# An adaLN block with a spectral mixer and a SwiGLU layer: more planes added on VectorE, a weight row loaded by itself, a split last tile, and new step orders

## The chip, the cores and the metric

The kernel runs on one core of one Trainium2 chip. Its time is the device time of one execution in microseconds, the median of several runs. The engines are named as in the profile: PE is TensorE (matmuls; PEld its weight loads), DVE is VectorE, ACT is ScalarE, POOL is GpSimd, and SP is SyncE, which here only issues transfers. Sixteen DMA engines move the data.

## The reference

The input x has 2048 tokens of 640 channels, in bf16. Six vectors of 640 (shift, scale and gate for two halves) come from a small condition vector c and a matrix w_mod.

```python
mod = (_silu(c) @ w_mod).reshape(c.shape[0], 6, 1, -1)      # sa, ca, ga, sb, cb, gb
h = _layernorm(x, axis=-1) * (1 + ca) + sa
X = rfft2(h over tokens and channels) * (w_r + 1j * w_i)     # w_r, w_i: 2048 x 321
x = x + ga * irfft2(X)
h = _layernorm(x, axis=-1) * (1 + cb) + sb
x = x + gb * ((_silu(h @ w_gate) * (h @ w_up)) @ w_down)     # 640 -> 1728 -> 640
```

## The kernel before

The tokens lie in 16 tiles t of 128. The work is one straight program. Within each stage a string, the plan, lists the steps, and the order of that list is the order in which each engine gets its instructions; engines run their own queues in order and wait for one another by semaphores. The plans were written out ahead of time. A step is a letter and a number: `S12` is the step S for tile 12.

**First stage (functions under ps1, to about 35 us).** For each tile t: `T` turns x on PE (x_sb is loaded in pairs of tiles by `lx`), `h` copies the turned tile out of PSUM, `G` and `d` compute the norm's sums, `p`, `r` and `s` the scaled Fourier table (POOL), `B` and `Z` the channel transform, `S` (s1) the first step of the token transform, and `A` (acopy) copies its result to A_sb; A12 is copied in three pieces. Which engine copies is set by the names in ON_DVE: named ones go to DVE, the others to ACT. `lca`, `ca`, `cb` and `rs` handle the scale ca, `lsa`, `ms`, `sacs`, `mh` and `sh` the shift sa. Before the first T, PE runs small matmuls on c and 12 matmuls on an identity tile (L400).

**The spectral weights.** Wb holds w_i in plane 0 and w_r in plane 1, as 128 partitions x 16 slots x 321 columns. `lW` (L223) loads one plane, `lf` (fix_rows, L210) then overwrites parts of partition 0 with other rows of the same matrix, and `J` (turn_w, L438) reads all of it on PE, reversed; `Je` (L443) copies that to Wq, and `N` makes the negated plane. `J2` and `J3` read w_i, `J0` and `J1` w_r:

```python
ws = [w.rearrange("(k2 k1) l -> k1 k2 l", k1=P) for w in (A_w_i, A_w_r)]
"lW": lambda a: nc.sync.dma_start(Wb[:, a, :, 0:321], ws[a])
nc.sync.dma_start(Wb[0:1, a, lo:hi, m:m + 63], ws[a][0:1, k:k + hi - lo, m:m + 63])   # lf
wv = Wb[:, 1 - h // 2, :, 1:257].rearrange("p k (m l) -> p k m l", m=2)               # J, step h
```

All these loads are issued by SP in the order of the plan: the x and G loads, `lsa`, `lW1`, `lW0`, `lK` (Ktab), the fix rows, `lga` (columns of the gate ga, wm_g), then the transposes `B`/`Bl` of A_sb by DMA.

**Second stage (to about 64 us).** 17 units u of four columns each. `T` and `t` turn units 0, 1 and 16 on PE (t2, L498; the others come by DMA transposes), `X` (stage_x) transforms, `Xe` copies out, `P` and `R` multiply by the weights on DVE (L562), giving two planes. For a unit in ADDED, `a` (add_planes, L570) adds the planes on DVE and `Y` turns the sum with 5 transposes (L580, L581); for the others `Y` adds and turns with 10 matmuls on an identity (L586, L590). `y` (L599) copies Y out, `E` transforms back, `e` (L634) copies to Ep, and `m` writes mirrored columns. ADDED is (0, 2, 4, 6, 8, 10, 12, 14).

**Third stage and FFN.** `s` (L720), `V`, `d`, `x` form x1, followed by the second norm and the turned tiles h2T. Then for each of four groups sc of four tiles: 13 blocks of `ffn_mm` (L812), silu on ACT, a product on DVE (ffn_mul, L821), and `down` (L934), which accumulates 13 blocks for each half of each tile, plus `down13`. `fold` (L848) multiplies a block of w_down by the gate gb on DVE; in the first group it runs between products, by the table `folds`.

**The last half tile** (sc 3, tl 3, h 1) uses two PSUM parts of 160 columns: x is added by two identity matmuls (L931), the 13 blocks go alternately to both parts, ACT copies one part and DVE the other (L946), and one store takes both.

Of the kernel before, what the change touches and what calls it, by code (L numbers as in the profile page):

```python
# [11 lines left out]
BF16 = mybir.dt.bfloat16  # L12
# [18 lines left out]
def _tables():  # L31
# [70 lines left out]
    "012021021021021020210210212012010210210210210"  # L102
)
SLOTS2 = (
    "0301321032103213012301230210321023102301230213201231032103210231023102310231320132012310321020130323"
    "013120132013201320132013201320132013201320132013201320132013201320132"
# [4 lines left out]
def adaln_block_kernel(  # L111
# [39 lines left out]
    one11 = const.tile([1, 1], BF16, name="one11")  # L151
    identb = const.tile([P, 128], BF16, name="identb")
# [29 lines left out]
    g_row = [dram.tile([1, D], BF16, name=n) for n in ("ga_row", "gb_row")]  # L182
    nc.vector.memset(one11[:], 1.0)
# [28 lines left out]
    def load(o, i):  # L212
        return lambda _: nc.sync.dma_start(o, i)
# [4 lines left out]
    def load_g(g):  # L218
# [4 lines left out]
             "lW": lambda a: nc.sync.dma_start(Wb[:, a, :, 0:321], ws[a]), "lK": load(Ktab[:], K_dram), "lKI": load(KIt[:], KI_dram),  # L223
# [3 lines left out]
        "A12 Xe0 Xe9 Xe10 Xe16 e1 e14 e15 f0 f1 f2 f3 f4 f6 f7 f8 f9 g15 h0 t0 t1 y0 y2 y4 y8 y12 y14 y16 "  # L227
# [55 lines left out]
    with tc.tile_pool(name="ph1", bufs=3) as ph1, \  # L283
# [111 lines left out]

        cps = Tt[:, 330:330 + NC5]
        for k in range(NC5):
            nc.tensor.matmul(cps[:, k:k + 1], lhsT=c_row[0:1, k * 128:(k + 1) * 128], rhs=one11[:], start=True, stop=True)
        for _ in range(12):
            nc.tensor.matmul(Gt[:, 0:128], lhsT=identb[:], rhs=identb[:], start=True, stop=True)  # L400
# [44 lines left out]
        def negate(i):  # L445
# [30 lines left out]
    with tc.tile_pool(name="ph2", bufs=2, reuse_waits="tile") as ph2:  # L476
# [186 lines left out]
        def loads(i):  # L663
# [11 lines left out]
        ADDED = (0, 2, 4, 6, 8, 10, 12, 14)  # L675
        MCOLS = ((0, 15), (15, 31), (31, 47), (47, 59), (59, 63))
        plan = (
# [30 lines left out]
    def ring(name):  # L708
        return take2(name)
# [109 lines left out]
    def ffn_mul(AT, fc):  # L819
        gu, sg = gus.pop(fc)  # L820
        nc.vector.tensor_tensor(AT[:, fc, :], gu[:, 1, :], sg[:], ALU.mult)  # L821
# [28 lines left out]
    def at_of(sc):  # L850
# [31 lines left out]
    folds = {8: (4, 5, 6), 9: (7,), 10: (8,), 11: (9, 10, 11), 12: (12, 13)}  # L882
    for sc in range(4):
        AT = at_of(sc)
        if sc:
            ffn13(sc)
        for fc in range(0 if sc else done, NFC - 1):
            ffn_mm(sc, fc)
            ffn_silu(fc)
            if sc == 0:  # L890
                for f in folds.get(fc, ()):
                    fold(f)
            ffn_mul(AT, fc)
            if fc == 2:
                ffn_mul13(sc, AT)
            if sc == 1 and fc == 4:
                ln2_power(8, 16)
            if sc < 3:
                n0 = 4 * (sc + 1)
                if fc in (9, 10):  # L900
                    ln2_xn(n0 + 2 * (fc - 9))
                    ln2_xn(n0 + 2 * (fc - 9) + 1)
                if fc == 10:
                    ln2_turn(sc + 1)
        if sc < 3:
            ln2_affine(sc + 1)
        acc = [t_[:, h, 0:320] for t_ in [ring("oa") for tl in range(4)] for h in range(2)]
        if sc == 3:
            acc[7] = [ring("ob")[:, 0, 0:160] for _ in range(2)]

        def early(tl, h):
            return tl > 1 and not (sc == 3 and tl == 3 and h)

        def parts(tl, h):
            o = acc[2 * tl + h]
            return [(o[q], 160 * q, 160) for q in range(2)] if isinstance(o, list) else [(o, 0, 320)]

        def down13(tl, h):
            r = slice(64 * h, 64 * h + 64)
            for o, d0, n in parts(tl, h):  # L920
                nc.tensor.matmul(o, lhsT=AT[r, 13, tl * 128:(tl + 1) * 128], rhs=Wd_sb[r, 13, h * 320 + d0:h * 320 + d0 + n],
                                 start=early(tl, h), stop=not early(tl, h))

        def x_half(tl, h):
            return x1[:, 4 * sc + tl, 320 * h:320 * h + 320]

        def down(tl, h):
            ps = parts(tl, h)
            if len(ps) > 1:
                for o, d0, n in ps:  # L930
                    nc.tensor.matmul(o, lhsT=identb[:], rhs=x_half(tl, h)[:, d0:d0 + n], start=True, stop=False)  # L931
            for fc in range(NFC - 1):
                for o, d0, n in ps:
                    nc.tensor.matmul(o, lhsT=AT[:, fc, tl * 128:(tl + 1) * 128], rhs=Wd_sb[:, fc, h * 320 + d0:h * 320 + d0 + n],  # L934
                                     start=(fc == 0 and not early(tl, h) and len(ps) == 1), stop=(fc == NFC - 2 and early(tl, h)))

        xos = {}

        def x_out(tl, h):
            t = 4 * sc + tl  # L940
            if h == 0:
                xos[tl] = ph4.tile([P, D], BF16, name="xo", bufs=3)
            ps = parts(tl, h)
            if len(ps) > 1:
                for (o, d0, n), copy in zip(ps, (nc.scalar.copy, nc.vector.tensor_copy)):
                    copy(xos[tl][:, h * 320 + d0:h * 320 + d0 + n], o)  # L946
            else:
                nc.vector.tensor_tensor(xos[tl][:, h * 320:(h + 1) * 320], ps[0][0], x_half(tl, h), ALU.add)  # L948
            if sc == 3 and tl == 3:
                nc.sync.dma_start(out_v[:, t, h * 320:(h + 1) * 320], xos[tl][:, h * 320:(h + 1) * 320])  # L950
            elif h == 1:
                nc.sync.dma_start(out_v[:, t, :], xos[tl][:])

        for tl in range(2):
            for h in range(2):
                down(tl, h)
        for tl in range(4):
            for h in range(2):
                if tl < 2 or early(tl, h):
                    down13(tl, h)  # L960
        for tl in range(2):
            for h in range(2):
                x_out(tl, h)
        for tl in range(2, 4):
            for h in range(2):
                down(tl, h)
                if not early(tl, h):
                    down13(tl, h)
                if sc == 3 and tl == 3:
                    x_out(tl, h)  # L970
            if sc < 3 or tl == 2:
                for h in range(2):
                    x_out(tl, h)
# [48 lines left out]
```

## Time and profile before

| What | us |
|---|---|
| median of 3 runs | 263.67 (262.97 to 264.32) |
| the profiled execution | 262.81 |
| its span | 261.0 |
| PE busy | 252.7 (97% of the span) |
| DVE busy | 141.1 (54%) |
| ACT busy | 118.6 (45%) |
| POOL busy | 26.4 (10%) |

The span runs from the first to the last instruction in the trace. In the rows of groups the numbers behind the count are busy us, the mean of one in ns, and the idle time before them with what ended it. A row of the timeline has its start, its length, engine, line and operation; a row of the chain has start, length and what it was. Shares are means over stages with different limits, so the stages are read one by one.

### The profile page before, as it was taken

To read this page: it belongs to the slowest core of one execution; us is meant where nothing else is said; L and a number is where in the kernel's file an instruction comes from. 1 tells how busy PE (TensorE), PEld (TensorE's weight loads), DVE (VectorE), ACT (ScalarE), POOL (GpSimd) and SP (SyncE) were. 2 spreads that over 40 slices of the span, in tenths; PEclk is the share of its full clock that TensorE was granted. 3 is DMA by queue.
4 is the path that set the end of the run, shared out by engine and by line. 5 is a ranking of instruction groups with operands and counts; after the bars stand their busy time and mean duration, and the time that the engine had idled before them with its cause. 6 is when DMAs were issued, how large, how long until landed. Compare 5 with 4: busy or idle time off the path is not lost.

```text
span 261.0 us, 5283 instructions
## 1 busy us (share of the span) xinstructions
PE 252.7 (97%) x2168; PEld 159.9 (61%) x2172; DVE 141.1 (54%) x353; ACT 118.6 (45%) x212; POOL 26.4 (10%) x57
## 2 busy tenths in 40 slices
PE   6899999999999999999999999999999999999995
PEld 5788666888995444466544456744445664444664
DVE  5799989999887664933243343234344322433122
ACT  5689879996993669420222222032223103222000
POOL 4289700000010001300000000000000000000000
PEclk9999999999999999999999999999999999999999
DMA  7999499999599100141100040210005011000011
GB/s 243 381 356 298 112 175 160 176 330 379 153 370 303 38 14 1 23 77 57 58 10 3 0 92 11 75 35 10 3 0 100 30 48 35 10 3 0 0 53 50
DMA packets 36798, 27.88 MB, mean 107 GB/s; under 512 B 19493, under 2 KB 34214, under 8 KB 36646
## 3 DMA queue, kind: packets, MB, share of 16 engines
q1 hardware_dynamic: 36762, 27.54, 37.1%
q8 instruction: 17, 0.28, 0.5%
q14 instruction: 7, 0.06, 0.1%
q10 hardware_dynamic: 12, 0.00, 0.0%
HBM read 20.13 MB, written 2.62 MB: 87 GB/s over the span
## 4 chain that ended last, share of the span: by engine, by line
PE 79%; DVE 12%; ACT 3%; issue 2%; DMA 2%; SPq 1%; DVEq 0%; ACTq 0%
PE gu L812 37%; PE oa L934 21%; PE va L720 3%; DVE PP L562 3%; DMA x_sb<-in_A_x_dram 2%; PE oab L733 2%; PE gu L799 2%; ACT junk L744 2%; PE aps L353 1%; DVE AT L821 1%; PE aps L354 1%; PE z L340 1%; DVE Z L345 1%; PE gps L308 1%; DVE late L848 1%
## 5 line engine op out<-in xcount | busy, mean ns | idle before, releaser
L821 DVE TENSOR_TENSOR AT<-gu,sg 128x512 bf16<-128x512 f32 x52 | 35.7, 690 | 63.3 <-ACT sg L817 63.3
L812 PE MATMUL gu<-h2T_all,Wg 128*128 128x512 bf16 x260 | 64.6, 379 | 0.1
L812 PE MATMUL gu<-h2T_all,Wu 128*128 128x512 bf16 x256 | 63.7, 379 | 0.1
L817 ACT ACTIVATE sg<-gu 128x512 f32<-128x512 f32 x52 | 30.7, 596 | 67.9 <-PE gu L812 65.1
L934 PE MATMUL oa<-late,AT 128*128 128x320 bf16 x403 | 56.3, 299 | 0.5 <-DVE AT L821 0.5
L934 PEld LDWEIGHTS <-AT 128*128 128x128 bf16 x429 | 40.7, 98 | 17.6 <-issue 1.1
L812 PEld LDWEIGHTS <-Wu 128*128 128x128 bf16 x260 | 25.4, 98 | 30.7
L812 PEld LDWEIGHTS <-Wg 128*128 128x128 bf16 x260 | 25.3, 98 | 29.9
L948 DVE TENSOR_TENSOR xo<-oa,late 128x320 bf16<-128x320 f32 x31 | 13.4, 484 | 34.6 <-PE oa L934 18.2
L801 ACT ACTIVATE sg<-gu 64x512 f32<-64x512 f32 x4 | 2.4, 591 | 36.0 <-PE gu L799 36.0
L736 DVE SCALAR_TENSOR_TENSOR late<-oab,x_sb 128x640 bf16<-128x640 f32 x16 | 12.8, 822 | 6.4 <-PE oab L733 5.0
L333 POOL TENSOR_SCALAR Gs<-Gtab,rstd 128x256 bf16<-128x256 bf16 x15 | 13.9, 928 | 8.1 <-DVE rstd L323 7.1
L345 DVE SCALAR_TENSOR_TENSOR Z<-rtile,vm,z 128x640 bf16<-128x640 f32 x16 | 13.9, 871 | 0.1
L744 ACT ACTIVATE junk<-late,mean 128x640 bf16<-128x640 bf16 x16 | 13.3, 828 | 0.3
L367 ACT CAST A_sb<-aps 128x650 bf16<-128x650 f32 x15 | 10.6, 706 | 2.1 <-PE aps L354 2.0
L727 ACT CAST VT<-va 128x640 bf16<-128x640 f32 x16 | 10.2, 699 | 1.9 <-PE va L720 1.8
L720 PE MATMUL va<-Htab,Ep 128*128 128x128 bf16 x160 | 10.6, 219 | 0.1
L720 PEld LDWEIGHTS <-Ep 128*128 128x128 bf16 x160 | 9.5, 118 | 0.4 <-DVE Ep L278 0.3
L353 PE MATMUL aps<-Z,Gs 128*128 128x325 bf16 x32 | 9.2, 303 | 0.2 <-DVE Z L345 0.2
L354 PE MATMUL aps<-Z,Gs 128*128 128x315 bf16 x32 | 9.2, 298 | 0.0
L540 ACT CAST X<-xps 128x640 bf16<-128x640 f32 x13 | 8.5, 710 | 1.1 <-PE xps L531 0.8
L562 DVE TENSOR_TENSOR PP<-X,Wb 128x768 bf16<-128x768 bf16 x16 | 8.7, 550 | 0.0
(291 smaller groups left out, 307.0 us busy)
## 6 DMA issues: line engine op xcount, KB each, us to landing
x_sb<-in_A_x_dram SPq DMA_DIRECT2D x8, 320.0 KB
out_dram<-xo SPq DMA_DIRECT2D x15, 160.0 KB, 2.2
Wu<-in_B_w_up_dram SPq DMA_DIRECT2D x1, 2080.0 KB
late<-in_B_w_down_dram SPq DMA_DIRECT2D x1, 2080.0 KB
wm_g<-in_w_mod_dram SPq DMA_DIRECT2D x2, 800.0 KB
Wb<-in_A_w_r_dram SPq DMA_DIRECT2D x1, 1284.0 KB
Wb<-in_A_w_i_dram SPq DMA_DIRECT2D x1, 1284.0 KB, 13.0
Wg<-in_B_w_gate_dram SPq DMA_DIRECT2D x1, 1280.0 KB, 8.1
```

The costliest lines, as they stand in the source:

```text
L333: e.tensor_scalar(Gss[t][:, 0:2], Gtab[:, t], rstd1[:, t:t + 1], None, ALU.mult)
L345: nc.vector.scalar_tensor_tensor(Zs[t][:].rearrange("p r q -> p (r q)"), rv, vm[:, t, 1:2], held.pop(("z", t))[:, 0:D], ALU.mult, ALU.add)
L353: nc.tensor.matmul(o, lhsT=Gs[:, a, :], rhs=Z[:, :, 0:NL], start=True, stop=False)
L562: nc.vector.tensor_tensor(bass.AP(o.tensor, o.offset, [o.ap[0], [4 * NI, 2], [2 * NI, 2], [4, n], [1, 4]]), bass.AP(xi.tensor, xi.offset, ...
L720: nc.tensor.matmul(vf[:, 128 * r:128 * r + 128], lhsT=Ep[:, t, 65 - 65 * g:193 - 65 * g, r], rhs=Htab[:, t, g, :], start=(f == 1 and r in ...
L736: nc.vector.scalar_tensor_tensor(x1[:, t, :].rearrange("p (a r) -> p a r", r=NR), VTs.pop(t).rearrange("p (r a) -> p a r", r=NR), 1.0, x_s ...
L744: nc.scalar.activation(junk[:], x1[:, t, :], ACT.Square, scale=-1.0 / D ** 0.5, bias=mean2[:, t, 1:2], accum_out=sq2[:, t:t + 1])
L812: nc.tensor.matmul(o, lhsT=w_[:, c5, fc * 128:(fc + 1) * 128], rhs=h2T(sc, c5), start=(c5 == 0), stop=(c5 == NC5 - 1))
L817: nc.scalar.activation(gus[fc][1][:], gus[fc][0][:, 0, :], ACT.Silu)
L821: nc.vector.tensor_tensor(AT[:, fc, :], gu[:, 1, :], sg[:], ALU.mult)
L934: nc.tensor.matmul(o, lhsT=AT[:, fc, tl * 128:(tl + 1) * 128], rhs=Wd_sb[:, fc, h * 320 + d0:h * 320 + d0 + n], start=(fc == 0 and not ear ...
L948: nc.vector.tensor_tensor(xos[tl][:, h * 320:(h + 1) * 320], ps[0][0], x_half(tl, h), ALU.add)
```

## The change

Eleven units are in ADDED: 1, 5, 9 and 13 come in, 0 goes out. ON_DVE changes: A11 in place of A12, h3 in place of h0; of the second stage's copies Xe0, Xe9, Xe10, Xe16, e1, e14 and the first half of e15 go to ACT, and the y copies of added units except y8 go to DVE. A tile `hot` is zeroed first on DVE, and PE runs 11 matmuls on it before the small ones on c and 11 after (instead of 12 on the identity). `lw` loads partition 0 of a weight plane, and `lW` the other 127. The folds of blocks 12 and 13 follow the last product of the first group, and the others are spread anew. The last half tile is computed part by part: each part takes its 13 blocks and down13, one DVE operation that adds x, and its own store; no identity matmuls. The three plans and the orders of the PSUM slots are new.

```diff
+    hot = const.tile([P, 128], BF16, name="hot")
+    nc.vector.memset(hot[:], 0.0)
...
-             "lW": lambda a: nc.sync.dma_start(Wb[:, a, :, 0:321], ws[a]), ...
+             "lw": lambda a: nc.sync.dma_start(Wb[0:1, a, :, 0:321], ws[a][0:1]),
+             "lW": lambda a: nc.sync.dma_start(Wb[1:P, a, :, 0:321], ws[a][1:P]), ...
...
-        "A12 Xe0 Xe9 Xe10 Xe16 e1 e14 e15 f0 f1 f2 f3 f4 f6 f7 f8 f9 g15 h0 t0 t1 y0 y2 y4 y8 y12 y14 y16 "
+        "A11 f0 f1 f2 f3 f5 f6 f7 f8 f9 g15 h3 t0 t1 y1 y2 y4 y5 y6 y9 y10 y12 y13 y14 y16 "
...
+        def keep_busy(n):
+            for _ in range(n):
+                nc.tensor.matmul(Gt[:, 0:128], lhsT=hot[:], rhs=hot[:], start=True, stop=True)
+        keep_busy(11)
         for k in range(NC5):
             nc.tensor.matmul(cps[:, k:k + 1], lhsT=c_row[0:1, k * 128:(k + 1) * 128], rhs=one11[:], start=True, stop=True)
-        for _ in range(12):
-            nc.tensor.matmul(Gt[:, 0:128], lhsT=identb[:], rhs=identb[:], start=True, stop=True)
+        keep_busy(11)
...
         plan = (    # first stage, the end of it
-            ... lg14 ... lsa ... lW1 ... lW0 ... lK ... lf0 ... lf7 ... B15 ms4 p14 r14 A10 ms1 A12 S13 Z15 J3 wm s15 A13 S15 J2 s14 sacs
-            N1 Je3 A15 N0 mh S14 sh Je2 J0 N2 A14 J1 Je1 Je0
+            ... lg14 lw1 ... lw0 ... lsa lW1 ... lW0 ... lK ... lga ... lf4 ... lf7 ... lKI ... lRi ... B15 J2 wm Je2 s13 ms4 r14 Z15 S12 ms1 s15 S13 s14
+            sacs A12 N1 S15 J3 A13 mh lf2 N0 S14 A15 Je3 sh A14 lf3 N2 J0 Je0 J1 Je1
...
-        ADDED = (0, 2, 4, 6, 8, 10, 12, 14)
+        ADDED = (1, 2, 4, 5, 6, 8, 9, 10, 12, 13, 14)
...
-    folds = {8: (4, 5, 6), 9: (7,), 10: (8,), 11: (9, 10, 11), 12: (12, 13)}
+    folds = {8: (4, 5), 9: (6, 7), 10: (8, 9), 11: (10, 11), 13: (12, 13)}
...
             ffn_mul(AT, fc)
+            if sc == 0 and fc == NFC - 2:
+                for f in folds[13]:
+                    fold(f)
...
         def parts(tl, h):
-            o = acc[2 * tl + h]
-            return [(o[q], 160 * q, 160) for q in range(2)] if isinstance(o, list) else [(o, 0, 320)]
+            k = 2 * tl + h
+            return [(acc[k], 0, 160, True), (acc[8], 160, 160, False)] if k == 7 and sc == 3 else [(acc[k], 0, 320, tl > 1)]
...
+            nc.vector.tensor_tensor(xos[tl][:, d0:d0 + n], o, x1[:, t, d0:d0 + n], ALU.add)
             if sc == 3 and tl == 3:
+                nc.sync.dma_start(out_v[:, t, d0:d0 + n], xos[tl][:, d0:d0 + n])
...
+                for part in parts(tl, h):
+                    down(tl, h, part)
+                    if not part[3]:
+                        down13(tl, h, part)
+                    if sc == 3 and tl == 3:
+                        x_out(tl, h, part)
```

Before, lga stood at the start of the second stage's plan, and lKI and lRi inside it. The order of the x and G loads ahead of lg14 is the same.

More of the change, by code (lines that the diff above doesn't have):

```diff
@@ L101 @@
 SLOTS1 = (
-    "012021021021021020210210212012010210210210210"
+    "012021021021021021020120121021201201201201201"
 )
 SLOTS2 = (
-    "0301321032103213012301230210321023102301230213201231032103210231023102310231320132012310321020130323"
-    "013120132013201320132013201320132013201320132013201320132013201320132"
+    "0310321032130210230123012031230123102310230123013201231023102103201320130231032103210310213021230231"
+    "03203210321032103210321032103210321032103210321032103210321032103210"
 )
@@ L222, in adaln_block_kernel @@
              "lca": lambda i: nc.sync.dma_start(wm_ca[:, 4 * i:4 + i], wm_v[:, 4 * i:4 + i, D:2 * D]),
-             "lW": lambda a: nc.sync.dma_start(Wb[:, a, :, 0:321], ws[a]), "lK": load(Ktab[:], K_dram), "lKI": load(KIt[:], KI_dram),
+             "lw": lambda a: nc.sync.dma_start(Wb[0:1, a, :, 0:321], ws[a][0:1]),
+             "lW": lambda a: nc.sync.dma_start(Wb[1:P, a, :, 0:321], ws[a][1:P]), "lK": load(Ktab[:], K_dram), "lKI": load(KIt[:], KI_dram),
              "lga": load(wm_g[:, :, 0:D], wm_v[:, :, 2 * D:3 * D]), "lRi": load(Rinv_sb[:], Rinv_dram), "lf": fix_rows}
     ON_DVE = set((
-        "A12 Xe0 Xe9 Xe10 Xe16 e1 e14 e15 f0 f1 f2 f3 f4 f6 f7 f8 f9 g15 h0 t0 t1 y0 y2 y4 y8 y12 y14 y16 "
+        "A11 f0 f1 f2 f3 f5 f6 f7 f8 f9 g15 h3 t0 t1 y1 y2 y4 y5 y6 y9 y10 y12 y13 y14 y16 "
     ).split())
@@ L908, in adaln_block_kernel, with down13, down, x_out @@
         if sc == 3:
-            acc[7] = [ring("ob")[:, 0, 0:160] for _ in range(2)]
-        def early(tl, h):
-            return tl > 1 and not (sc == 3 and tl == 3 and h)
+            acc[7] = acc[7][:, 0:160]
+            acc.append(ring("ob")[:, 0, 0:160])
         def parts(tl, h):
-            o = acc[2 * tl + h]
-            return [(o[q], 160 * q, 160) for q in range(2)] if isinstance(o, list) else [(o, 0, 320)]
[L918 to L931, printed above, removed]
+            k = 2 * tl + h
+            return [(acc[k], 0, 160, True), (acc[8], 160, 160, False)] if k == 7 and sc == 3 else [(acc[k], 0, 320, tl > 1)]
+        def down13(tl, h, part):
+            r, (o, d0, n, early) = slice(64 * h, 64 * h + 64), part
+            nc.tensor.matmul(o, lhsT=AT[r, 13, tl * 128:(tl + 1) * 128], rhs=Wd_sb[r, 13, h * 320 + d0:h * 320 + d0 + n],
+                             start=early, stop=not early)
+        def down(tl, h, part):
+            o, d0, n, early = part
             for fc in range(NFC - 1):
-                for o, d0, n in ps:
-                    nc.tensor.matmul(o, lhsT=AT[:, fc, tl * 128:(tl + 1) * 128], rhs=Wd_sb[:, fc, h * 320 + d0:h * 320 + d0 + n],
-                                     start=(fc == 0 and not early(tl, h) and len(ps) == 1), stop=(fc == NFC - 2 and early(tl, h)))
+                nc.tensor.matmul(o, lhsT=AT[:, fc, tl * 128:(tl + 1) * 128], rhs=Wd_sb[:, fc, h * 320 + d0:h * 320 + d0 + n],
+                                 start=(fc == 0 and not early), stop=(fc == NFC - 2 and early))
         xos = {}
-        def x_out(tl, h):
+        def x_out(tl, h, part):
             t = 4 * sc + tl
@@ L942, in x_out @@
                 xos[tl] = ph4.tile([P, D], BF16, name="xo", bufs=3)
[L943 to L948, printed above, removed]
+            o, d0, n, _ = part
+            d0 += 320 * h
+            nc.vector.tensor_tensor(xos[tl][:, d0:d0 + n], o, x1[:, t, d0:d0 + n], ALU.add)
             if sc == 3 and tl == 3:
-                nc.sync.dma_start(out_v[:, t, h * 320:(h + 1) * 320], xos[tl][:, h * 320:(h + 1) * 320])
+                nc.sync.dma_start(out_v[:, t, d0:d0 + n], xos[tl][:, d0:d0 + n])
             elif h == 1:
@@ L955, in adaln_block_kernel @@
             for h in range(2):
-                down(tl, h)
+                down(tl, h, parts(tl, h)[0])
         for tl in range(4):
             for h in range(2):
-                if tl < 2 or early(tl, h):
-                    down13(tl, h)
+                down13(tl, h, parts(tl, h)[0])
         for tl in range(2):
             for h in range(2):
-                x_out(tl, h)
+                x_out(tl, h, parts(tl, h)[0])
         for tl in range(2, 4):
             for h in range(2):
[L966 to L970, printed above, removed]
+                for part in parts(tl, h):
[4 more added lines that the diff above has]
+                        x_out(tl, h, part)
             if sc < 3 or tl == 2:
                 for h in range(2):
-                    x_out(tl, h)
+                    x_out(tl, h, parts(tl, h)[0])
 @with_exitstack
```

34 rows, old and new, of the table plan are left out of this document.

## The prediction

> **What bounds the kernel now.** I read the page first, then busy time by stage, then the chain of work that ended last, then the transfers. From the page and from a table of stages that I cut where the chain changes its lines (columns: length, busy us and count of PE, PEld, DVE, ACT, POOL, clock, transfer share, GB/s):
>
> ```profile
> span 261.0 us, 5283 instructions
> 14.50:34.30 19.80, 19.47 (x262) 15.90 (x260) 19.00 (x62) 17.23 (x31) 15.65 (x26) 1.00 0.81 243
> 34.30:64.20 29.90, 28.71 (x455) 23.35 (x452) 28.74 (x69) 25.98 (x44) 0.00 (x0) 1.00 1.01 245
> 125.65:169.67 44.02, 44.02 (x248) 23.58 (x247) 15.51 (x29) 10.46 (x17) 0.00 (x0) 1.00 0.14 34
> ```
>
> The two transform stages fill every engine; in the second, DVE (28.74 of 29.90 us) is as full as PE. From 64 us on it is PE's stream of matmuls, and nothing of the change shortens that stream but its ends. The chain shows where a transfer counts at all:
>
> ```profile
> 2.66 4.79 DMA x_sb<-in_A_x_dram
> 7.50 0.49 PE t L301 x5
> ...
> 35.22 0.32 PE t2ps L498 x5
> ```
>
> Only the second pair of x rows is on it. The spectral weights, which the change cuts into two transfers each, are not on it: they land in time. So the question for them is how much time is left. From the transfer view, the queue of SP, and the instructions on Wb:
>
> ```profile
> Wb<-in_A_w_i_dram SPq DMA_DIRECT2D x1, 1284.0 KB, 13.0
> 13.12 5.61 SPq L223 DMA_DIRECT2D Wb<-in_A_w_i_dram  x1
> 18.77 3.61 SPq L213 DMA_DIRECT2D Ktab<-tab_K  x1
> 26.23 2.58 SPq L210 DMA_DIRECT2D Wb<-in_A_w_i_dram  x4
> 0.00:16.90 16.90, 13.71 (x181) 11.77 (x182) 11.77 (x48) 11.34 (x21) 8.15 (x29) 1.00 0.93 324
> 16.90:24.80 7.90, 7.90 (x111) 6.98 (x110) 7.59 (x28) 7.28 (x14) 7.54 (x12) 1.00 1.12 346
> 56.00:64.00 8.00, 7.90 (x115) 6.90 (x112) 8.00 (x20) 6.62 (x12) 0.00 (x0) 1.00 1.03 408
> L438 PE MATMUL wps<-Wb,jrev x8: 384/384/397, 30.6 to 34.8; 128*128 128x512 bf16 x8
> ```
>
> What is queued ahead of the weights is, by its shapes, x 2560 KB, G 1024, the scale columns 800, R 160 and the shift columns 800, together 5344 KB or 5.47 MB; 324 GB/s over 16.9 us is 5.48 MB, the same: the weights start at 16.9 us. All sixteen engines carry them, at 346 GB/s, 21.6 GB/s each; the second (the planes are alike, 1284 KB each) lands at 13.12 + 13.0 = 26.1 us. Its fix rows, which wait for that, are issued from 26.23 for 2.58 us, and the first reader on PE, L438, starts at 30.6. With partition 0 loaded alone the fix rows no longer wait for the plane, so the plane itself would have 30.6 - 26.1 = 4.5 us to spare, and more than that the change cannot draw from it: PE has no gap at that place.
>
> **The row loaded alone.** This is the part that I take to decide. `lw` moves partition 0 (16 runs of 642 bytes; two more issues on SP, whose queue there waits for transfers anyway: nothing). `lW` then moves partitions 1 to 127, and 127 is prime. Does the split over the engines need equal shares of the rows? The trace has one row on this, the queue that ACT issues on:
>
> ```profile
> q10 hardware_dynamic: 12, 0.00, 0.0%
> first_w<-in_c_dram ACTq DMA_DIRECT2D x1, 1.2 KB
> ga_row<-gTa ACTq DMA_DIRECT2D x1, 1.2 KB
> DMA packets 36798, 27.88 MB, mean 107 GB/s; under 512 B 19493, under 2 KB 34214, under 8 KB 36646
> ```
>
> Two transfers, one of a single row (c) and one of five (ga): 6 data packets, and 12 in all, so one closing packet for each share: 1 and 5 engines, not 16. The packets under 512 B come out to the unit in the same way: transposes 16,640, the gate and up tails 1,280, single rows 74, and 1,499 closing packets, if each copy of 128 or 64 rows is closed 16 times, the 15-row ones 15, the 5-row ones 5, one-row ones once, and the 12 transposes 32 times each (this last fitted). Every transfer of this kernel is cut into equal shares of its outer rows. 127 rows have only one equal share. An uneven cut (fifteen engines with 8 rows and one with 7) never occurs here, so the trace cannot exclude it; but it would be the first of its kind. I take one engine.
>
> The Trainium skill says so outright ("DMA: Bandwidth & Descriptors", section on why a DMA increments its semaphore by 16): the engine count is the largest up to 16 that divides the outer size of both sides, and 127 partitions give 1. The packet counts agree for 1, 5, 15 and 128 rows; no run here shows 127.
>
> Price: 2 x 1284 KB x 127/128 = 2.609 MB through one engine. At its present 21.6 GB/s that takes 120.8 us. Bounds: an engine alone could go as fast as with the long rows of the up weights, 408/16 = 25.5 GB/s (102.3 us), or be slower by the overlap in the share of 1.12, 19.3 GB/s (135.2 us). I take 21.6, the row of these very runs. So the weights end at 16.9 + 120.8 = 137.7 us. Behind them in that engine's line stand its sixteenths of Ktab and of the ga columns (192 + 800 KB)/16 = 62 KB, 2.9 us, and then the fix rows that the first reader also waits for. SP is held meanwhile: the rows above show it stopped 5.61 and 3.61 us when much is outstanding, so Ktab and all later issues stand behind both weights. With about 1 us to land (an estimate from 26.1 against 24.8, where the row of 346 GB/s ends), the first reader, now J2, starts at 141.6 us.
>
> PE runs in order, and ahead of J2 stand all steps through B15; behind it S12, S13, S15, J3, the shift's transform, S14, J0, J1. So everything waits. From the first L438 to the first turn T0 (t2ps) it took 35.2 - 30.6 = 4.6 us before. After a stop it is longer, because ACT's copies no longer run ahead:
>
> ```profile
> L443 ACT CAST Wq<-wps 128x1024 bf16<-128x1024 f32 x4 | 4.0, 1019 | 0.2 <-PE wps L438 0.2
> L367 ACT CAST A_sb<-aps 128x650 bf16<-128x650 f32 x15 | 10.6, 706 | 2.1 <-PE aps L354 2.0
> L362 DVE CAST A_sb<-aps 128x325 bf16<-128x325 f32 x1 | 0.5, 500 | 0.3 <-PE aps L354 0.3
> 3.94 0.73 PE L301 MATMUL t1ps<-identb,x_sb 128*128 128x128 bf16 x5
> 7.50 0.75 PE L301 MATMUL t<-identb,x_sb 128*128 128x128 bf16 x10 [0.28 <-DMA x_sb<-in_A_x_dram]
> ```
>
> Je2 and Je3 at 1.02, A13, A15 and A14 at 0.71, and A12 (three pieces, on DVE before, the largest 0.50; I take 1.2 for all) are 5.4 us; J2 itself on a cold PE about 0.9 us (five transposes took 0.73 us at 3.94 and ten took 0.75 at 7.50, so PE starts at about half its rate). T0 comes at 141.6 + 0.9 + 5.4 = 147.9 us, against 35.2: **112.7 us late**. Below nothing it cannot be, since nothing else may go ahead of J2 on PE.
>
> The Trainium skill's clock rule ("TensorE: Matmul & The Clock Gate", Part 1) gives half rate after an idle window of about 3.4 us and full rate after as long a busy one, so at most 1.7 us lost after the stop: by it the sum would be under 1 us more. The two rows of transposes above agree with it.
>
> **Eleven added planes, other copies.**
>
> ```profile
> L570 DVE TENSOR_TENSOR PP<-PP 128x640 bf16<-128x640 bf16 x8 | 3.7, 482 | 0.0
> L586 PE MATMUL yps<-identb,PP 128*128 128x128 bf16 x66 | 5.2, 220 | 0.0
> L599 ACT CAST Y<-yps 128x640 bf16<-128x640 f32 x8 | 5.7, 738 | 0.0
> L599 DVE COPY Y<-yps 128x640 bf16<-128x640 bf16 x6 | 2.9, 486 | 0.3 <-PE yps L581 0.3
> L540 ACT CAST X<-xps 128x640 bf16<-128x640 f32 x13 | 8.5, 710 | 1.1 <-PE xps L531 0.8 <-ACT B L504 0.3
> L540 DVE CAST X<-xps 128x640 bf16<-128x640 f32 x3 | 2.5, 822 | 0.8 <-PE xps L531 0.7
> L536 DVE CAST X<-xps 128x160 bf16<-128x160 f32 x1 | 0.3, 314 | 0.0
> L634 DVE CAST Ep<-eps__1131 128x640 bf16<-128x640 f32 x1 | 0.8, 827 | 0.1
> L634 ACT CAST Ep<-eps__1145 128x640 bf16<-128x640 f32 x1 | 0.7, 721 | 0.4 <-PE eps__1145 L624 0.4
> 46.10 0.45 PE yps L586 x8
> ```
>
> DVE gains three additions (1.45) and four Y copies net (1.94), and gives three X copies (2.47), Xe16 (0.31), e1 and e14 (1.65) and half of e15 (half an e1, 0.4) to ACT: about 1.4 us less, 27.3 of 29.9. ACT takes three X copies at 0.71, two and a half E copies at 0.72 and Xe16, 4.2 us, and has six Y copies where it had ten, 2.9 less: 27.3. PE saves five matmuls of 0.45/8 us in each of three units, 0.84: 27.9. So the fullest engine falls from 28.74 to 27.9, by 0.9 us. Bounds: 1.4 gained, if DVE alone sets the pace, or 1.3 lost, if ACT does, which now also waits on longer chains (an addition stands before each of eleven Y). I take 0.9 gained.
>
> **Plans, folds, tail, start.**
>
> ```profile
> PE oa L934 <- DVE AT L821: 0.5, 1, 0.5
> 255.78 0.30 PE L931 MATMUL ob<-late,identb 128*128 128x160 bf16 x2
> 255.91 1.96 PE L934 MATMUL ob<-late,AT 128*128 128x160 bf16 x26
> 256.49 2.38 SPq L950 DMA_DIRECT2D out_dram<-xo  x2
> 258.15 0.33 DVE L946 CAST xo<-ob 128x160 bf16<-128x160 f32 x1 [1.69 <-PE ob L921]
> 2.39 1.46 PE L400 MATMUL gps<-identb 128*128 128x128 bf16 x12
> ```
>
> The folds of 12 and 13 now follow DVE's last product of the first column of tokens; PE waited 0.5 us for that product: 0 to 0.5 gained, I take 0.5, since down needs fold 12 only at its 13th matmul. In the tail the two identity matmuls go (255.78 to 255.91, 0.13), the first 160 columns are added and stored under the second part's 14 matmuls, and the last store carries half as much behind one DVE operation as long as before: 0 to 0.4, I take 0.2; SP issues one store more, the last still behind the last sum. At the start eleven fillers on a zeroed tile (about 1.3 us by L400) run in PE's wait for c, and eleven instead of twelve in its wait for x; the chain's x transfer until 7.45 hides all of it, so nothing; uncovered, 0.2 lost or, by an earlier full clock, 0.3 gained. The order in the first stage: PE has 19.47 us of work in 19.80, so nothing.
>
> **The sum.** The profiled execution took 262.81 us, 1.8 outside its span and 0.9 under the median of 263.67. 262.81 + 112.7 - 0.9 - 0.5 - 0.2 = 373.9: **374 us**.
>
> **Rivals.** *The weights still go through sixteen engines*, by an uneven cut or a cut of the runs: nothing is late, and 262.81 - 1.6 = 261.2 us, faster. For it: nothing on 127 rows in the trace. Against it: the equal shares in every packet count. The point that decides is the engine count: the load takes 120.8/k us and may last the present 7.9 plus the 4.5 to spare plus the gain of 1.6, so from nine engines up it is faster, and 127 gives no number between one and sixteen. *The same, but ACT eats the second stage's gain* (27.3 us of work plus longer chains, 0.3 lost there): 262.81 + 0.3 - 0.7 = 262.4, no change.
>
> **The numbers.** What this measurement can tell from no change is about 0.5%, 1.3 us. One engine: 0.87, all slower. Sixteen: 0.08 faster (261.2), 0.04 the same (262.4); 0.01 for ACT's loss in full, slower. The range is that of the first case: 102.3 and 135.2 us in place of 120.8 give 355 and 388; J2 to T0 and the second stage add about 4 to each side: 350 to 392, left only with a tenth of that case: 0.87 x 0.92 = 0.80.
>
> **What would show it.** Right: the changed kernel's L445 (turn_w) starts near 141 us, PE idle for some 110 us before it with a Wb load as releaser, GB/s near 22 from 17 to 138 us, SP held over 50 us in L226; then the second stage within 29 us and no 0.5 us wait at the first down. Wrong: Wb lands before 31 us at some 346 GB/s; then the time is near 261, and the equal-share step has failed. If L445 starts well off 141, it is the rate of one engine.

## The result

The changed kernel takes 377.24 us (median of 6 runs, 376.11 to 377.91) where the kernel before took 263.34 beside it (6 runs, 262.97 to 264.32): 1.4315 times as long, interval 1.4283 to 1.4346. The forecast was 374 us, in a range of 350 to 392. Its profiled execution took 376.95 us, with a span of 375.2.

The page of the changed kernel, first line, the granted clock and the GB/s in 40 slices of 9.4 us:

```profile
span 375.2 us, 5272 instructions
...
PEclk9996555555555556999999999999999999999999
...
GB/s 283 307 25 23 22 22 22 22 22 22 22 22 22 22 166 62 161 253 330 179 373 39 10 43 56 51 7 2 70 37 42 9 0 70 54 24 9 0 12 60
```

Some 110 us at 22 GB/s and half clock. SP's queue shows what was on the way (start, us in the issue):

```profile
13.77 0.41 SPq L226 DMA_DIRECT2D Wb<-in_A_w_r_dram  x1
14.23 59.58 SPq L226 DMA_DIRECT2D Wb<-in_A_w_i_dram  x1
73.85 59.66 SPq L215 DMA_DIRECT2D Ktab<-tab_K  x1
...
134.11 2.66 SPq L212 DMA_DIRECT2D Wb<-in_A_w_i_dram  x4
```

and the table of stages (length, busy us and count of PE, PEld, DVE, ACT, POOL, clock, transfer share, GB/s) how many engines carried it: a share of 0.07 is 1.1 of 16.

```profile
25.00:80.00 55.00, 4.66 (x66) 3.87 (x63) 6.26 (x17) 4.89 (x9) 6.27 (x10) 0.56 0.07 22
80.00:135.00 55.00, 0.00 (x0) 0.00 (x0) 0.00 (x0) 0.00 (x0) 0.00 (x0) 0.50 0.08 25
```

PE's timeline of the changed kernel has the stop at J2 (L445), then the starts of T0 (L505), of the first `va` after the second stage (L727) and of the down matmuls of the last column of tokens (L935). The idle time before an instruction stands in brackets with its releaser.

```profile
142.03 1.01 PE L445 MATMUL wps<-Wb,jrev 128*128 128x512 bf16 x2 [112.37 <-DMA Wb<-in_A_w_i_dram]
...
149.83 0.72 PE L505 MATMUL t2ps<-identb,A_sb 128*128 128x128 bf16 x10
...
177.81 2.43 PE L727 MATMUL va<-Htab,Ep 128*128 128x128 bf16 x40
...
356.19 7.23 PE L935 MATMUL oa<-late,AT 128*128 128x320 bf16 x52
```

The same three points in the kernel before:

```profile
35.08 0.61 PE L498 MATMUL t2ps<-identb,A_sb 128*128 128x128 bf16 x8
...
63.65 2.15 PE L720 MATMUL va<-Htab,Ep 128*128 128x128 bf16 x30
...
242.66 7.23 PE L934 MATMUL oa<-late,AT 128*128 128x320 bf16 x52
```

They cut both spans into four parts. The columns "whole planes" and "mended" are two of the experiments below, cut at the same instructions.

| part, us | before | changed | whole planes | mended |
|---|---|---|---|---|
| start to T0 | 35.08 | 149.83 | 35.90 | 36.58 |
| T0 to the first `va` (second stage) | 28.57 | 27.98 | 28.10 | 28.14 |
| to the last column's down | 179.01 | 178.38 | 178.38 | 178.04 |
| from there to the end | 18.34 | 19.01 | 18.82 | 18.34 |
| span | 261.0 | 375.2 | 261.2 | 261.1 |

The 114.2 us more in the span are 114.75 ahead of T0, 0.59 and 0.63 won behind it, and 0.67 lost at the end.

### The profile page after: what moved, and what is told of

It reads as the page before. It is cut to its first block, busy times and chain, and to the rows that moved or that the text cites. A ratio compares the mean times of both kernels' runs of the same rounds, so it can differ in the third digit from the quotient of the medians.

```text
span 375.2 us, 5272 instructions
## 1 busy us (share of the span) xinstructions
PE 254.8 (68%) x2161; PEld 161.4 (43%) x2165; DVE 139.8 (37%) x353; ACT 119.4 (32%) x216; POOL 26.6 (7%) x57
## 4 chain that ended last, share of the span: by engine, by line
PE 51%; DVE 1%; issue 0%; ACT 0%
PE gu L819 30%; PE oa L935 15%; PE va L727 2%; PE gu L806 1%; PE oab L740 1%; PE oa L929 1%; PE mg_ps L244 0%; PE h2ps L779 0%; PE ob L935 0%; DVE late L743 0%; DVE xo L946 0%; ACT sg L824 0%; DVE late L855 0%; PE ob L929 0%; PE gT_ps L256 0%
## 5 line engine op out<-in xcount | busy, mean ns | idle before, releaser
L445 PE MATMUL wps<-Wb,jrev 128*128 128x512 bf16 x8 | 3.1, 502 | 112.4 <-DMA Wb<-in_A_w_i_dram 112.4
L819 PE MATMUL gu<-h2T_all,Wu 128*128 128x512 bf16 x260 | 64.6, 379 | 0.2
L819 PE MATMUL gu<-h2T_all,Wg 128*128 128x512 bf16 x256 | 63.7, 379 | 0.1
L935 PE MATMUL oa<-late,AT 128*128 128x320 bf16 (+1 forms) x416 | 57.3, 297 | 0.8 <-DVE xo L946 0.6
L445 PEld LDWEIGHTS <-jrev 128*128 128x128 bf16 x8 | 0.8, 112 | 113.1 <-DMA Rinv_sb<-tab_Rinv 112.5
L935 PEld LDWEIGHTS <-AT 128*128 128x128 bf16 x429 | 40.8, 98 | 18.0 <-issue 2.1
L421 DVE TENSOR_SCALAR sacs<-Ktab,t1ps 128x100 bf16<-128x100 bf16 x5 | 1.1, 297 | 113.1 <-PE t1ps L416 113.1
L450 ACT CAST Wq<-wps 128x1024 bf16<-128x1024 f32 x4 | 4.0, 1018 | 112.9 <-PE wps L445 112.9
L946 DVE TENSOR_TENSOR xo<-oa,late 128x320 bf16<-128x320 f32 (+1 forms) x32 | 13.8, 480 | 36.2 <-PE oa L935 19.4
L547 ACT CAST X<-xps 128x640 bf16<-128x640 f32 x16 | 10.3, 700 | 1.0 <-PE xps L538 0.9
L370 ACT CAST A_sb<-aps 128x650 bf16<-128x650 f32 x14 | 9.6, 704 | 2.8 <-PE aps L357 2.8
```

Of the source, the lines that this page charges most:

```text
L370: copy(o[:, :, at:at + 10].rearrange("p l (c r) -> p l c r", c=2), i)
L547: evict("Xe%d" % u)(Xs[u // 2][:, u % 2].rearrange("p q (b j) -> p q b j", b=2), xps[:, :, 0:2 * NI].rearrange("p b (j q) -> p q b j", j=2))
L819: nc.tensor.matmul(o, lhsT=w_[:, c5, fc * 128:(fc + 1) * 128], rhs=h2T(sc, c5), start=(c5 == 0), stop=(c5 == NC5 - 1))
L946: nc.vector.tensor_tensor(xos[tl][:, d0:d0 + n], o, x1[:, t, d0:d0 + n], ALU.add)
```

## The experiments

The theory was the prediction's: 127 rows have one equal share, so one engine carries each plane. The rivals: something else of the new plans holds J2; or any row count that 16 does not divide goes to one engine.

**The row alone, in the kernel before.**

```diff
-"lW": lambda a: nc.sync.dma_start(Wb[:, a, :, 0:321], ws[a]),
+"lw": lambda a: nc.sync.dma_start(Wb[0:1, a, :, 0:321], ws[a][0:1]),
+"lW": lambda a: nc.sync.dma_start(Wb[1:P, a, :, 0:321], ws[a][1:P]),
-... lg14 h6 T9 ...
+... lg14 lw1 lw0 h6 T9 ...
```

> The kernel before with one thing of the change: row 0 of each plane loaded alone, after the last G load, and the plane's 127 other rows as one load, at the old place in the old plan. Theory: all of the 112 us comes from here, so 262.8 + 112 = 375 us, at most 5 off, with SP held some 60 us in the issue of the second plane. Rival (the new plan, in which the planes stand elsewhere in SP's queue and ACT copies more, is part of it): well under 370.

Measured: 374.09 us, span 372.3. SP is held as in the changed kernel:

```profile
15.33 59.72 SPq L224 DMA_DIRECT2D Wb<-in_A_w_i_dram  x1
75.09 59.67 SPq L213 DMA_DIRECT2D Ktab<-tab_K  x1
```

The load cut in this way costs 374.09 - 263.03 = 111 of the 114 us (a single run) in the old plan; the new plans are not needed for it.

**The 127 rows cut evenly.**

```diff
-"lW": ... dma_start(Wb[1:P, a, :, 0:321], ws[a][1:P]),
+"lW": ... [dma_start(Wb[p0:p1, a, :, 0:321], ws[a][p0:p1]) for p0, p1 in ((1, 113), (113, P))],
```

> The changed kernel with the 127-row load of each plane cut in two, partitions 1 to 112 (16 equal shares) and 113 to 127 (15); all else as changed. Theory (equal shares alone cost the 112 us): the planes land before PE needs them, the stop at J2 goes, and the time is 262 to 263 us. By the prediction's terms for the rest it would be 261.2; by what the trace of the changed kernel shows of them (start 0.55 late, second stage 1.1 less, folds 0.1 less, tail 0.7 more) 262.8. Rival (the new plans themselves hold J2, or SP's queue does): over 370 still.

Measured: 271.75 us (270.09 to 272.72, 6 runs), 1.0323 times the kernel before, interval 1.0288 to 1.0358. More than 105 of the 114 us are gone, so the theory holds in the main; but 9 us stay, and none of the times in the expectation was met. PE still stops at J2, and the table of stages shows a slow load with every engine busy (the row is 18 to 26 us; share 1.15, 239 GB/s):

```profile
18.00:26.00 8.00, 8.00 (x107) 6.91 (x105) 7.75 (x29) 6.63 (x13) 8.00 (x15) 1.00 1.15 239
```

```profile
35.21 1.01 PE L445 MATMUL wps<-Wb,jrev 128*128 128x512 bf16 x2 [5.75 <-DMA Rinv_sb<-tab_Rinv]
```

(The profile names the transfer that ended last; what J2 reads are the weights and their fix rows.) The single row does what it was meant for: the fix rows are issued at 26.28, right behind the gate columns, where the run with 112 + 16 rows and no row alone, below, holds them till 33.31.

**124 rows and 126 rows.** As the changed kernel, with `4:P` and `0:4`, then `2:P` and `0:2`, in place of `1:P` and `0:1`.

> The changed kernel with four rows loaded alone and 124 in the large load, which 4 divides and no greater number up to 16. Theory of equal shares: four engines, 2.547 MB at 4 x 21.6 = 86.4 GB/s are 29.5 us, from 16.9 to 46.4; the first reader starts at 49 to 51 and the time is about 284 us; GB/s near 90 in the slices from 25 to 45 us. Rival (a row count that 16 doesn't divide falls back to one engine): 376.

> The changed kernel with two rows loaded alone and 126 in the large load, which 14 divides. Theory of equal shares: fourteen engines, 2.588 MB at 302 GB/s are 8.6 us, inside the time to spare: 262 to 263.5 us, as with the even cut. Rival (one engine for every count that 16 doesn't divide): 376.

Measured: 301.64 and 273.36 us. Not 376, so the rival of one engine for every count that 16 does not divide is out, and the times and shares fit four and fourteen engines. But both are late, by 18 and by 10 us. From the tables of stages, first of 124 rows, then of 126:

```profile
24.00:40.00 16.00, 5.62 (x75) 4.62 (x72) 7.18 (x20) 5.30 (x10) 7.16 (x12) 0.74 0.27 67
40.00:52.00 12.00, 0.00 (x0) 0.00 (x0) 0.00 (x0) 0.00 (x0) 0.00 (x0) 0.50 0.29 68
```

```profile
18.00:26.00 8.00, 8.00 (x107) 6.95 (x105) 7.75 (x29) 6.60 (x13) 8.00 (x15) 1.00 1.02 201
```

A share of 0.29 is 4.6 engines (the share reads high: it was 1.12 when sixteen engines carried the load), and 68 / 4 = 17 GB/s each; fourteen engines get 201 / 14 = 14.4 each. One engine alone had 22, sixteen in the kernel before 346 / 16 = 21.6. The number of engines follows equal shares; what each of them moves does not stay the same.

The packet counts say the same to the unit. The queue of SP, in the kernel before, in the changed one, and with the even cut:

```profile
q1 hardware_dynamic: 36762, 27.54, 37.1%
```

```profile
q1 hardware_dynamic: 36908, 27.54, 25.2%
```

```profile
q1 hardware_dynamic: 36968, 27.54, 37.1%
```

The last column's store in two parts adds 128 + 16 = 144 packets; the two planes were closed by 2 x 16 and now are by 2 x 1, and the two single rows by 2 x 16, one for each of their 16 runs: 144 + 2 = 146, as counted. With the even cut 2 x 31 + 2 x 16 closings give 36968, with 124 rows 2 x 4 + 2 x 4 give 36890, with 126 rows 2 x 14 + 2 x 2 give 36906: all three are what the pages count. The changed kernel's count alone would also fit sixteen closings for each plane and one for each row; the even cut decides, since of its 94 closings the parts of the planes can take 62 at most in shares of 16 and 15, which leaves 32 for the two rows.

**Whole planes again, new plans kept.** This parts the rate from the plan.

```diff
-"lw": ...,  "lW": ... two parts ...
+"lW": lambda a: nc.sync.dma_start(Wb[:, a, :, 0:321], ws[a]),
-"lw1 h7 B3 lw0 h9 s0 ...
+"h7 B3 h9 s0 ...
```

> The changed kernel with both planes loaded whole on 128 partitions, as before, and no row alone; the new plans and all else stay. After the even cut still stopped PE 5.8 us at J2, two theories are left. Rate: the 112 + 15 rows went at 195 to 290 GB/s between 18 and 32 us where whole planes had gone at 345, because their shares do not lie on the partitions as the shares of 128 rows do; then whole planes land by 25, the stop at J2 falls to under 1 us, and the time is 262.8 to 264 us. Plan: the new plan has 800 KB of gate columns ahead of the fix rows that J2 waits for; if that is the cause, J2 still waits 3 us or more and the time is 266 to 270.

Measured: 262.81 us (262.36 to 264.09, 12 runs), 0.9989 times the kernel before, interval 0.9963 to 1.0014: no change. Table of stages and PE's timeline:

```profile
18.00:26.00 8.00, 8.00 (x107) 6.92 (x105) 7.79 (x30) 6.59 (x14) 8.00 (x14) 1.00 1.10 334
```

```profile
30.64 0.61 PE L445 MATMUL wps<-Wb,jrev 128*128 128x512 bf16 x2 [1.09 <-DVE rstd L326]
```

The rate theory was right: 334 GB/s, and a time at the low end of its range; the stop of 1.1 us is slightly over the forecast of under 1. So the cut of the load costs the changed kernel 377.24 - 262.81 = 114.4 us, and all other parts of the change together are worth nothing that can be measured.

**Gate columns behind the fix rows, with the even cut.** `lga` is moved in the first plan from ahead of `s4` to behind `lf3`.

> The even cut (112 + 15 rows, row 0 alone) with the 800 KB of gate columns moved in the plan from ahead of the fix rows to behind the last of them, where the kernel before had them too. If the queue's order made the 5.8 us stop at J2: J2 starts under 30.5 and the time is 263 to 264 us. If the slow load did: 800 KB at 220 GB/s are 3.7 us, so J2 starts at 31.5 and the time is 266 to 268. If neither: 271 to 272 as it was.

Measured: 267.61 us; the stop at J2 is 3.2 us, and it starts at 32.83:

```profile
32.83 1.01 PE L445 MATMUL wps<-Wb,jrev 128*128 128x512 bf16 x2 [3.23 <-DMA Wb<-in_A_w_i_dram]
```

J2 starts 2.4 us earlier than with the even cut alone. The time is in the range of the slow-load theory (266 to 268), but J2 was to start at 31.5: 800 KB take 3.4 us at 239 GB/s, and not all of that came back. So the order made part of the stop, and a stop of 3.2 us is left that the order does not explain. With whole planes the same move left J2 where it was (31.23 against 31.33, two runs below).

**What makes the load slow.** Three cuts of whole planes, no row alone: `((0, 112), (112, 128))`, `((0, 64), (64, 128))`, and all rows in two halves of the sixteen column blocks, `Wb[:, a, k:k + 8, 0:321]` for k = 0 and 8.

> As the run with whole planes, but each plane in two loads, partitions 0 to 111 (16 shares of 7 rows) and 112 to 127 (16 shares of 1). Every engine has 8 rows of each plane, as with whole planes, and both loads start at a multiple of 16. If it is the place of the shares on the partitions that slows the load (several engines at once on one group of partitions): GB/s of 200 to 290 again between 18 and 30 us, J2 at 33 to 35.5, 267 to 272 us. If it was the start at partition 1, the fifteen shares or the single row alone: as with whole planes, within 1 us.

> As the run with whole planes, but each plane in two loads of 64 partitions, 16 shares of 4 rows each. Bytes, runs and rows for each engine are as with whole planes, starts are round; only which rows each engine has differs: in half a plane sixteen engines write to 64 partitions. The Trainium skill (SBUF - State Buffer, section on the DMA port swizzle) gives 64 partitions half the ports of 128 and 196 GB/s for them against 328. If the place of the rows decides, the load goes at 200 to 300 GB/s, ends 3 to 6 us later than whole planes, and the time is 3 to 8 us over that run; if only the number of shares does, it is within 1 us of it.

> As the run with whole planes, but each plane in two loads of all 128 partitions, eight of its sixteen column blocks each: as many loads as in the runs with 112 + 16 rows and with two halves, and the same bytes, runs and shares. If the place of each engine's rows on the partitions made those two slow: GB/s of 310 to 350 between 18 and 26 us and 262.5 to 263.5 us. If the second load did (more issues, more closings): 265 or more.

Measured: 271.33, 275.12 and 263.19 us. The rows of the tables of stages, for 112 + 16 rows, for halves of 64, and for column halves:

```profile
18.00:26.00 8.00, 8.00 (x107) 6.93 (x105) 7.79 (x29) 6.59 (x14) 8.00 (x14) 1.00 1.16 199
```

```profile
18.00:26.00 8.00, 8.00 (x106) 6.90 (x105) 7.79 (x29) 6.58 (x13) 8.00 (x14) 1.00 1.18 165
```

```profile
18.00:26.00 8.00, 8.00 (x105) 6.86 (x104) 7.79 (x29) 6.59 (x13) 8.00 (x14) 1.00 1.11 342
```

The halves cost 12.3 us over whole planes, more than the 3 to 8 expected, and with 112 + 16 rows J2 came at 37.3, later than the 33 to 35.5 expected. All three have sixteen engines, the same bytes and runs, and two loads for each plane. Only those that change which rows an engine has are slow: 199 and 165 against 342 and 334. Halves of 64 rows go at half the rate (165 / 334 = 0.49). So an engine's rate hangs on where its rows lie beside the other engines' rows; that is shown. What they share there is not, nor whether it lies on the side of the partitions or of the source, where each engine's rows change as well. The Trainium skill names a candidate ("SBUF — State Buffer", section on the DMA port swizzle): sixteen ports of eight partitions each, to which 64 partitions have access through eight only, 196 GB/s against 328; and "DMA: Bandwidth & Descriptors", on the descriptor swizzle, has each engine of a 128-row transfer write one port. Eight ports of sixteen are a half, with which 165 / 334 = 0.49 agrees, better than with the page's own 196 / 328 = 0.60; no run here shows a port.

**The small stops mended.** The trace of the changed kernel shows three, which I mended on top of whole planes. In its tail (PE, then DVE):

```profile
370.05 1.06 PE L935 MATMUL oa<-late,AT 128*128 128x160 bf16 x13 [0.58 <-DVE xo L946]
```

```profile
369.50 0.49 DVE L946 TENSOR_TENSOR xo<-oa,late 128x320 bf16<-128x320 f32 x1 [0.88 <-PE oa L935]
```

The last half tile's first part lies in the same slot as `acc[6]`, and PE waits till DVE has read that one. At the first down matmuls (DVE, then PE):

```profile
224.62 0.69 DVE L828 TENSOR_TENSOR AT<-gu,sg 128x512 bf16<-128x512 f32 x1 [1.23 <-ACT sg L824]
225.22 0.88 DVE L855 TENSOR_TENSOR late<-late,gb_bc 128x640 bf16<-128x640 bf16 x2
```

```profile
223.79 1.79 PE L935 MATMUL oa<-late,AT 128*128 128x320 bf16 x12
225.76 3.42 PE L935 MATMUL oa<-late,AT 128*128 128x320 bf16 x24 [0.18 <-DVE late L855]
```

DVE sits idle for 1.23 us ahead of its last product, and the folds stand behind it. At the start, the fillers wait for DVE's last setup write, into the tile they overwrite, so the matmuls on c come at 3.11, where they came at 2.17 before:

```profile
1.84 1.33 PE L401 MATMUL gps<-hot 128*128 128x128 bf16 x11 [1.84 <-DVE gps L293]
3.11 0.29 PE L406 MATMUL t1ps<-one,first_w 1*128 1x1 bf16 x5
```

```diff
-folds = {..., 11: (10, 11), 13: (12, 13)}
+folds = {..., 11: (10, 11), 12: (12, 13)}
-            if sc == 0 and fc == NFC - 2: ...
-acc[7] = acc[7][:, 0:160]
+acc[7] = ring("ob")[:, 0, 0:160]     # and its 14th matmul behind the other 13
+nc.vector.memset(Gt[:, 130:131], 1.0)  # now ahead of neg1, hT_all, ssq
```

> The run with whole planes and three mends of what the trace of the changed kernel showed. The last half tile's first part gets a PSUM slot of its own instead of the other half of the slot that DVE is still reading: the 0.58 us stop of PE goes, the tail from the last wide down matmul group on is 18.2 us or less instead of 18.85. Folds 12 and 13 stand ahead of DVE's last product, in which DVE sits idle for 1.23 us, instead of behind it: the first down matmuls are not late for them, 0.3 to 0.6 us. The constant that the first filler matmuls wait for is written first: the shift of 0.5 us at the start goes, which was hidden behind the G loads and so is worth nothing. Sum: 0.9 to 1.2 us under the run with whole planes, 261.6 to 261.9. Rival (the stops only move: the slot is late for another reason, the folds delay the product that they overtake): within 0.3 us of it.

Measured: 262.63 us (261.69 to 264.67, 12 runs), 0.9974 times the kernel before, interval 0.9943 to 1.0004. By its trace each mend did what it should: in the table above the tail is 18.34 instead of 18.82 and the stretch with the folds 178.04 instead of 178.38. PE's timeline:

```profile
2.36 0.29 PE L406 MATMUL t1ps<-one,first_w 1*128 1x1 bf16 x5
...
31.33 0.61 PE L445 MATMUL wps<-Wb,jrev 128*128 128x512 bf16 x2 [1.82 <-DVE Gs L337]
...
255.87 1.06 PE L932 MATMUL ob<-late,AT 128*128 128x160 bf16 x13
```

But J2 starts 0.69 us later than in the run with whole planes, at 31.33, and T0 with it; that eats the 0.8 us won. By the trace PE's weight load for J2 waits for the fix rows in both runs (1.2 us with whole planes, 2.0 here), and these are issued when the plane has landed:

```profile
26.84 2.75 SPq L208 DMA_DIRECT2D Wb<-in_A_w_i_dram  x4
```

With whole planes alone the first fix row had gone out at 26.94, no earlier than here, and J2 could start sooner all the same; why is not shown. (The releasers in brackets, `rstd` and `Gs` on DVE, are not the cause: J2 reads neither, and DVE runs both at the same times in the two runs.) Over the profiles of these kernels and of the column halves the first fix row goes out between 26.6 and 27.9 us. Two runs tried to get round it, both on the mended kernel: the gate columns behind the fix rows, and J2 behind S12 and ms1 in PE's order.

> The same three mends, and the 800 KB of gate columns issued behind the last fix row instead of ahead of the first. With whole planes PE still waited 1.1 us at J2, for fix rows that are issued behind those 800 KB (2.4 us at 334 GB/s). Theory: the fix rows land 2 us earlier, J2 starts at 29.6, and the time is 0.5 to 1.1 us under the run with the mends alone, 260.6 to 261.2. Rival (the gate columns then come between the transposing transfers of the second stage and make these late): no gain, or up to 1 us lost.

> The run with whole planes and the three mends, with J2 put behind S12 and ms1 in PE's order instead of ahead of them (the order of the PSUM slots changed to fit). In that run PE still stopped 1.8 us at J2 (1.1 in the run without the mends), from 29.5 to 31.3, for fix rows of which the last was issued at 29.2. S12 and ms1 are 0.75 us of matmuls that need no weights. Theory (the fix rows' landing sets J2): J2 still starts at 30.6 to 31.3 but 0.75 us more of work lies ahead of it, so the time is 0.7 us under the run with the mends, 261.9, the best of these kernels and some 0.5% under the kernel before. Rival (Je2 then comes later to the slot that S15 needs, and PE stops there instead): no gain.

Measured: 265.9 us (264.8 to 267.63, 8 runs), 1.0092 with an interval of 1.0051 to 1.0134, and 262.94 us (262.61 to 263.82, 12 runs), 0.9979 with 0.9957 to 1.0001. The first expectation, that the fix rows would land 2 us earlier, was wrong: SP stands idle from 23 to 26.87 us until the plane lands, whatever is queued, so J2 starts at 31.23 as before. SP's queue, and the row of stages in which PE then falls to half clock:

```profile
19.41 3.62 SPq L211 DMA_DIRECT2D Ktab<-tab_K  x1
26.87 2.75 SPq L208 DMA_DIRECT2D Wb<-in_A_w_i_dram  x4
```

```profile
32.50:36.00 3.50, 3.50 (x24) 1.98 (x23) 2.64 (x7) 2.79 (x7) 0.00 (x0) 0.52 0.38 53
```

J2 to T0 then takes 6.9 us instead of 5.25. That explains 1.6 of the 1.8 us by which its profiled execution is longer; the other runs of that kernel were up to 2.8 us longer still, and no profile shows why. In the second the plane landed a microsecond later (27.93), J2 started at 31.93 behind a stop of 0.53, and the slot of S15 cost 0.55 more, which its rival had named:

```profile
33.65 0.30 PE L356 MATMUL aps<-Z,Gs 128*128 128x325 bf16 x1 [0.55 <-ACT Wq L450]
```

No version here is measurably faster than the kernel before.

## Why the prediction was right

**The load.** It held step by step. J2 was put at 141.6 us and started at 142.03; the rate of one engine was taken as 21.6 GB/s and is 22; SP was to be held over 50 us and was, twice. The two alternatives with a time near 262 fell with the result, and the single row in the kernel before (374.09) shows that the load alone does it. That one engine alone kept the rate it had among sixteen is in part luck: with four engines each moved 17 GB/s and with fourteen 14.4, both under the lowest rate that the prediction allowed for (19.3).

**J2 to T0** was mis-sized: 6.3 us forecast, 142.03 to 149.83 = 7.80 measured. With whole planes it takes 35.90 - 30.64 = 5.26, so the cold PE cost 2.5; the prediction had allowed for it only inside J2's own 0.9. The clock stayed at 0.50 until 147.9, 5.8 us after PE had work again, and PE's matmuls, not ACT's copies, filled the stretch. This and J2's 0.4 make T0 1.9 us later than forecast.

**The second stage**: 0.9 forecast, 28.57 - 27.98 = 0.59 won; with whole planes 0.47. **The folds**: 0.5 forecast. The stretch from the first `va` is 0.63 shorter, of which the stop at the first down gives 0.49 - 0.18 = 0.31; the rest is not placed. The stop did not go altogether: the folds now stand behind the last product, which DVE gets only after 1.23 us of idling, and the 13th matmul, the first to need one of them, comes 0.18 before it is done. **The tail** was wrong in sign: 0.2 forecast as won, 0.67 lost. I counted matmuls and the last store, and did not ask who still reads the slot into which the first part is written. **The start**: nothing forecast; T0's transposes of the first x rows come at 4.47 instead of 3.94, hidden before J2: with whole planes PE was ready for J2 at 29.55, and with the start mended at 29.51.

**The rival of sixteen engines** was priced at 261.2 us, faster. The run with whole planes comes nearest to that case, though its fix rows still wait for the plane, and took 262.81: the tail takes 0.5 of what was won, and T0 comes 0.8 later. The step of that rival that did not hold is "the 4.5 to spare": the new plan leaves PE ready for J2 at 29.5, and with whole planes J2 could start only at 30.6. And "from nine engines up it is faster" is refuted: fourteen gave 273.36, since it took the rate of an engine as fixed.

## What to carry to other kernels

Before a tile's load is cut by rows, work out two things: the greatest number up to 16 that divides the rows, which is how many engines carried it here (1 for 127 rows, 4 for 124, 14 for 126), and whether each engine keeps the rows it had in the load of 128; or cut by columns instead, which cost nothing here (342 GB/s against 334), where a cut by rows cost 8 to 12 us with all engines busy and 114 with one. In a trace, a transfer share near 1 with fewer GB/s than the neighbouring loads shows the second case, a share near 0.07 the first. And when an accumulator is moved into the free half of a slot, look for the reader of the other half.

## What the runs showed of the hardware

A single row of sixteen runs was closed sixteen times, so its runs were dealt to sixteen engines: in this load of one row the runs took the place of the rows. (The row c, a single run, was closed once.)

The clock of PE fell after short stops, and not always: with the even cut PE stopped at 29.5 and the clock was 0.50 from 31.0; in the mended kernel with the gate columns moved it fell at 32.6, after a stop of 1.78 us that had ended at 31.23; after the stop of 1.82 us in the mended kernel itself it stayed at 1.00, and with 126 rows it fell only at 34.2, 4.7 us after PE had stopped. After such a stop it came back 3.9 to 6.1 us behind the first new work. The Trainium skill ("TensorE: Matmul & The Clock Gate", Part 1) has it fall after an idle window of some 3.4 us, in windows that run free; the return agrees with one to two such windows, the fall after stops of 1.5 to 1.8 us does not, and the runs don't show what decides it.
